# Linear attention and a factored bilinear layer in one kernel: a second raw-weight buffer, placed decoding steps, and another split of transfers between two queues

## The chip, the cores and the metric

One core of one Trainium2 chip runs the whole program. The metric is the device time of one execution in microseconds (us); the median of several runs is compared. Beside it stands one execution taken with the hardware profiler, from which all rows below come. PE is the matrix engine (TensorE), PEld its weight loads, DVE the vector engine, ACT the scalar engine, POOL is GpSimd; SPq and POOLq are the instruction queues of SyncE and GpSimd, from which this kernel starts nearly all its DMAs.

## The reference

The inputs are float32: q, k, v of 8 batches x 8 heads x 576 positions x 64, the feature matrix w_phi (64 x 128), w_a and w_b (512 x 1536), w_out (1536 x 512). The maximum runs over the features of one position.

```python
def phi(x):
    proj = einsum('bhsd,df->bhsf', x, w_phi)
    proj = proj - max(abs(proj), axis=-1, keepdims=True)
    return concatenate([exp(proj), exp(-proj)], axis=-1)
q_p, k_p = phi(q), phi(k)
kv  = einsum('bhsf,bhsd->bhfd', k_p, v)
z   = sum(k_p, axis=2)
num = einsum('bhsf,bhfd->bhsd', q_p, kv)
den = einsum('bhsf,bhf->bhs', q_p, z)[..., None] + 1e-06
attn = num / den                      # 8 x 8 x 576 x 64
...
x = attn as 4608 tokens x 512
y = ((x @ w_a) * (x @ w_b)) @ w_out   # 4608 x 512
```

The three weight matrices come in as float64 values seen as integers: each raw tile holds 64-bit words, which the kernel decodes to float32 by itself.

## The kernel before

**Attention.** 32 steps, one for each pair of heads of a batch, run through a software pipeline: while pair i is projected (`project_first`, `project_last`), pair i-1 goes through `kv_products` and pair i-2 through `num_products` and `den_products`. ACT takes the exponentials (L138, L139, L173, L174) and the copies out of PSUM (`p` L152 and L165, `back` L198, `x` L216, `dn` L227). The normalised result goes to DRAM as `xnorm`.

**Decoding of weights.** `load_factors` treats one unit, a 256-row piece of w_a, w_b or w_out. There are 18 units: 9 for the first pass of what follows, which `early` decodes between the steps of attention, and 9 for the second pass, which `late` decodes during the first pass, from its second block on. A unit loads two raw tiles of 512 KB (`raw_00a` and so on: pass, quad, matrix; L323), one after the other into one buffer. Each is decoded by one ACT operation (L328) and four on DVE (L329, L331, L333, L335) into `w32`. Out of `w32` come the seven factors of a Winograd-like scheme (w11, w12, s2, s1, s3, w22, s4), each split into a high part (ACT, L87) and a low part (DVE, L88) in a tile `t` of two buffers, from which a DMA of 256 KB (L349) stores it to DRAM as `kept`. Loads and stores go through SyncE in the early half, through GpSimd in the late half. Of a decoding step, only this is fixed: it comes behind the last operation that was put in the list `marks`, which are DVE operations (`placed`). The rates DECODE_RATE and LAST_RATE say how many steps are drawn at each turn of attention and at each product of a pass.

**The two passes.** The second half computes y transposed, in two passes p over halves of the inner dimension. A pass goes over 6 blocks j of 768 tokens, a block over 3 quads q. For a quad, `winograd` does seven products for w_a and w_b, each of 6 matmuls for each of the two (two chunks, three products of high and low parts), and multiplies the two results; then `product` in `moe_block` does seven products with w_out, each of 3 matmuls for each quad and each half. That is 3 x 7 x 2 x 6 = 252 matmuls with w_a and w_b and 7 x 3 x 2 x 3 = 126 with w_out in a block, each of 128 x 128 by 384 columns: 378, and 4536 in all. Pass 0 stores its partial sums (`part`, L538) in DRAM, pass 1 loads them again (L532) and stores `out_x`.

**The ring.** Weight factors come back from `kept` in pairs of 512 KB (`back_w`, `back_s`, `back_o`; `fetch`, L374) into a ring of four tiles. Each fetch is drawn by `feed` behind a product and waits for the tile's earlier product. Of the 11 pairs of w_out factors of a pass, 10 stay on chip and one goes through the ring in each block, at its end. All those fetches, the loads of x (`xx`, L390), `part` and `out_x` go through SyncE, in the order of issue.

**What sets the order.** The Tile framework schedules every operation by an estimate of its own; `issue_after` (in `behind`) gives only a lower bound. On each engine and in each DMA queue the resulting order is then fixed, and a waiting instruction holds all that stand behind it.

Of the kernel before, what the change touches and what calls it, by code (L numbers as in the profile page):

```python
# [18 lines left out]
P = 128  # L19
# [6 lines left out]
DECODE_FROM, DECODE_RATE = 3, 1.22  # L26
X_FROM, X_RATE = 100, 0.8
LAST_FROM, LAST_RATE = 1, 1.45
# [7 lines left out]
def tile_kernel(ctx, tc, qP, km, kr, vm, vr, w_phi, eye, w_a, w_b, w_out, out):  # L36
# [56 lines left out]
    marks, loads, feeds, maxima, st = [], [], [], [], {}  # L93
# [35 lines left out]
    def features(u, y, n, a1, a2):  # L129

        p = y if n == NFULL else y[:, :, :F]
        p = p.rearrange("p j (c f) -> p j c f", f=F)
        d = a2.tile([P, 2, n, F], F32, tag=f"d{n}", name=f"d_{u}")
        m = a2.tile([P, 2, n], F32, tag=f"m{n}", name=f"m_{u}")
        nc.vector.tensor_reduce(out=m, in_=p, op=ALU.max, axis=AX.X, apply_absolute_value=True)
        marks.append(nc.vector.tensor_tensor(d, p, m.unsqueeze(3).broadcast_to([P, 2, n, F]), op=ALU.subtract))
        e = a1.tile([P, 2, n, 2, F], F32, tag=f"e{n}", bufs=2, name=f"e_{u}")
        nc.scalar.activation(e[:, :, :, 0], d, AF.Exp)  # L138
        nc.scalar.activation(e[:, :, :, 1], d, AF.Exp, scale=-1.0)  # L139
        return e  # L140
# [18 lines left out]
    def project_last(i, a1, a2, consts, duo):  # L159
        p32 = st["p", i]  # L160
        x = q_half(i, 1, consts, duo)
        if i % 2 == 0:
            for j in range(2):
                mm(x[:, j, HALF : HALF + F], st["rk", i][heads[j]], consts[0][heads[j]])
        nc.scalar.copy(p32[:, :, times[1]], x[:, :, :HALF])  # L165
        if i % 2 == 0:
            st["er", i] = st["er", i + 1] = features(f"r_{i}", x[:, :, HALF:], 1, a1, a2)
        eq = a1.tile([P, 2, 2, S], F32, tag="eq", bufs=3, name=f"eq_{i}")
        for j in range(2):
            mb = a2.tile([P, S], F32, tag="mb", name=f"mb_{i}_{j}")  # L170
# [3 lines left out]
        nc.scalar.activation(eq[:, :, 1], p32, AF.Exp, scale=-1.0)  # L174
        st["eq", i] = eq
# [125 lines left out]
    late_o = [(NQ - 1, k) for k in FACTORS[:2]]  # L301
    late_o += [(q, k) for k in FACTORS for q in range(NQ) if (q, k) not in late_o]
    outs = [[(p, q, "o", k) for q, k in late_o] for p in range(2)]
# [8 lines left out]
    def load_factors(p, q, nm):  # L312

        n = DM // 2
        w32 = coded.tile([P, 4, n], F32, tag="w32", name=f"w32_{p}{q}{nm}")
        w = w32.rearrange("p i n -> p (i n)")
        src = {"a": w_a, "b": w_b, "o": w_out}[nm]
        for i in range(2):
            f = 2 * (NQ * p + q) + i
            raw = coded.tile([P, DM, 2], U32, tag="raw", name=f"raw_{p}{q}{nm}{i}")  # L320
            queue = nc.gpsimd if p else nc.sync
            rows = src[f * P : (f + 1) * P, :].bitcast(U32)
            behind(maxima if p else [], lambda: queue.dma_start(raw.rearrange("p n w -> p (n w)"), rows))  # L323
            yield
            low, high = raw[:, :, 0], raw[:, :, 1]
            g, s = high.bitcast(F32), w[:, i * DM : (i + 1) * DM]
            gb, sb = g.bitcast(U32), s.bitcast(U32)
            nc.scalar.activation(g, high.bitcast(F32), AF.Prelu, scale=2.0**-112, alpha=2.0**32)  # L328
            nc.vector.tensor_scalar(sb, gb, 3, None, op0=ALU.logical_shift_left)  # L329
            yield  # L330
            nc.vector.tensor_scalar(gb, sb, 0xFF800000, None, op0=ALU.bitwise_and)  # L331
            yield
            nc.vector.scalar_tensor_tensor(g, low, 2.0**-52, g, op0=ALU.mult, op1=ALU.mult)  # L333
            yield
            nc.vector.tensor_tensor(s, s, g, op=ALU.add)  # L335
            yield
        at = dict(w11=0, w12=1, w21=2, w22=3)
        if nm == "o":
            at.update(w12=2, w21=1)

        def stored(*names):
            for k in names:
                key, place = two[p, q, nm, k]
                t = coded.tile([P, 2, n], F32R, tag="t", bufs=2, name=f"t_{p}{q}{nm}_{k}")
# [4 lines left out]
                queue.dma_start(kept[key][:, place], t.bitcast(F32))  # L349

        def sub(k, a, b, to, op=ALU.subtract):
            at[k] = at[to]
            nc.vector.tensor_tensor(w32[:, at[k]], w32[:, at[a]], w32[:, at[b]], op=op)

        stored("w11", "w12")
        yield
        stored("w22")
        yield
        sub("s1", "w21", "w22", "w22", op=ALU.add)
        stored("s1")  # L360
        yield
        sub("s3", "w11", "w21", "w21")
        sub("s2", "s1", "w11", "w11")
        yield
        stored("s3")
        sub("s4", "w12", "s2", "w12")
        yield
        stored("s2", "s4")
        yield

    def fetch(key, pool, tag, name):
        n = len(pairs[key])
        t = pool.tile([P, n, 2, DM // 2], F32R, tag=tag, name=f"back_{name}")
        feeds.append(nc.sync.dma_start(t.bitcast(F32), kept[key][:, :n]))  # L374
        weights[key] = t

    def factors_of_x(p, j, xs):
# [4 lines left out]
        for c in range(half):  # L382
# [3 lines left out]
            while t < (j + 1) * T:  # L386
# [3 lines left out]
                behind(feeds or loads, lambda: nc.sync.dma_start(x32[:, :, t0 : t0 + m], rows))  # L390
# [12 lines left out]
        for c in range(half):  # L403
            (x11, x12), (x21, x22) = ((t[:, :N], t[:, N:]) for t in (x[c], x[c + half]))
            sums = xin.tile([P, 2, N], F32, tag="xs", name=f"xs_{u}_{c}")
            t1, t2, t3, t4 = sums[:, 0], sums[:, 1], x12, x21
# [21 lines left out]
    def winograd(p, j, q, xs, hs, spaces, feed):  # L428
# [32 lines left out]
        def hi(k, src):  # L461
            hs[k] = [spaces["h"].tile([P, N], F32R, tag=f"h{part}_{q}_{k}", name=f"h{part}_{k}_{u}") for part in "hl"]
            nc.scalar.copy(hs[k][0], src)  # L463
# [30 lines left out]
        h21 = low[:, 1]  # L494
# [6 lines left out]
        t1, t2, t3, t4 = top0[:, 1], top1[:, 1], low[:, 0], top0[:, 0]  # L501
# [16 lines left out]
    def moe_block(p, j, xs, x_next, spaces, feed, spent):  # L518
# [9 lines left out]
        def given_tile(i, t):  # L528
            g = spaces["brief"].tile([P, 2, N], F32, tag=f"g{(0, 1, 2, 0)[2 * i + t]}", name=f"o_{p}_{j}_{i}{t}")
            given.update({(m, i, t): g[:, m] for m in range(2)})  # L530
            if p:
                behind(feeds, lambda: nc.sync.dma_start(g, src[:, i * (NCC // 2) : (i + 1) * (NCC // 2), t * N : (t + 1) * N]))  # L532
# [4 lines left out]
        def store(key):  # L537
            nc.sync.dma_start(dst[at(*key)], given[key])  # L538
# [21 lines left out]

        early, late_, every = range(NQ - 1), range(NQ - 1, NQ), range(NQ)
        for q in range(NQ):
            for _ in range(3 if q == 0 else 2):
# [4 lines left out]
                if q == 1:  # L568
                    next(x_next, None)
            if q < NQ - 1:  # L570
                next(quads[q + 1])
                if q == 1:
                    next(x_next, None)
# [7 lines left out]
            if q == 0:  # L581
                next(x_next, None)
            if q == 1:
                for i, t in ((0, 0), (0, 1), (1, 0)):
# [10 lines left out]
        spent()  # L595
# [24 lines left out]
        for m in range(2):  # L620
            product(m, "w22", 0, every)
            if p:
# [12 lines left out]
    def placed(steps):  # L635

        for _ in iter(lambda: behind(marks, lambda: done.append(next(steps, steps))), 0):
            if done.pop() is steps:
                return
            yield  # L640

    done = []
    units = [(p, q, nm) for p in range(2) for q in range(NQ) for nm in "ab"]
    units = [[u for u in units if u[0] == p] + [(p, q, "o") for q in range(NQ)] for p in range(2)]
    codes = [itertools.chain(*(load_factors(*u) for u in units[p])) for p in range(2)]
# [5 lines left out]
    order = deque(key for p in range(2) for _ in range(NB) for key in [(p, *key) for key in order] + [("o", p, 0)])  # L651
    ring, used = deque(f"ring{i}" for i in range(RING)), [0]

    def refill():
        key = order.popleft()
        fetch(key, ringed, ring[0], "_".join(map(str, (used[0], *key))))
# [12 lines left out]
    early, late = (placed(code) for code in codes)  # L669

# [21 lines left out]
    wouts = ctx.enter_context(tc.tile_pool(name="wouts", bufs=1))  # L692
    for p in range(2):
        own = deque(pair for pair in pairs if pair[:2] == ("o", p) and pair[2])

        def feed():
# [4 lines left out]
            if own and used[0] % 3:  # L701
                key = own.popleft()
                fetch(key, wouts, f"o{key[2]}", "_".join(map(str, key)))

# [3 lines left out]
        for j in range(NB):  # L708
            n_ = p * NB + j + 1
            x_next = factors_of_x(*divmod(n_, NB), xs) if n_ < 2 * NB else iter(())  # L710
            moe_block(p, j, xs, x_next, spaces, feed, lambda: refill() if order else None)
# [46 lines left out]
```

## Time and profile before

| | |
|---|---|
| median of 3 runs | 1321.12 us (1317.03 to 1327.0) |
| profiled execution, whole | 1316.53 us |
| its span in the trace | 1314.4 us |
| attention, about | 0 to 418 us |
| pass 0, about | 418 to 864 us |
| pass 1, about | 864 to 1312 us |
| PE busy | 1156.3 us (88%) |
| DVE / ACT / POOL busy | 929.7 / 632.9 / 187.1 us (71 / 48 / 14%) |
| TensorE clock granted, mean | 0.963 of 2.4 GHz |

The span runs from the first to the last instruction that the profiler shows; 2.1 us of the execution lie around it. Busy shares are means over three stages that differ.

### The profile page before, as it was taken

How to read it: one execution, taken by the hardware profiler on the slowest of the kernel's cores; microseconds unless marked ns; L12 is line 12 of the kernel's file. 1: busy time of each engine (PE TensorE's matmuls, PEld its weight loads, DVE VectorE, ACT ScalarE, POOL GpSimd, SP SyncE). 2: the span in 40 equal slices, each digit the busy share in tenths (PEclk: the TensorE clock that was granted, in tenths of full speed). 3: DMA queues.
4: the chain of work that ended last, by engine and by line, in shares of the span. 5: the costliest groups of instructions: out<-in, count | busy, mean ns of one | idle time of the engine just before them, and what ended most of it. 6: DMA issues, size and time to landing. Idle time of an engine off the chain costs nothing. (4 is left out here: it accounts for less than half of the span.)

```text
span 1314.4 us, 22642 instructions
## 1 busy us (share of the span) xinstructions
PE 1156.3 (88%) x8418; PEld 1005.5 (76%) x8418; DVE 929.7 (71%) x1774; ACT 632.9 (48%) x1239; POOL 187.1 (14%) x149
## 2 busy tenths in 40 slices
PE   8787878787878789798898989989998999898998
PEld 5454545444545689798898889889998999898998
DVE  6776677678973475977959597865858585767655
ACT  6665557566754243544535354443525352433432
POOL 4333244233321000111101111100000000000000
PEclk9998899889999899999999999999999999999999
DMA  6576565667552966868777787979676777768573
GB/s 205 184 242 201 168 201 176 190 191 218 174 162 88 334 223 216 304 217 307 257 256 258 246 294 265 322 238 315 205 246 225 229 252 217 244 199 270 179 216 126
DMA packets 131645, 297.77 MB, mean 227 GB/s; under 512 B 22800, under 2 KB 53904, under 8 KB 131536
## 3 DMA queue, kind: packets, MB, share of 16 engines
q1 hardware_dynamic: 123600, 270.24, 62.9%
q0 software_dynamic: 7632, 25.96, 5.3%
q8 instruction: 67, 1.10, 0.4%
q14 instruction: 42, 0.34, 0.1%
q10 hardware_dynamic: 304, 0.13, 0.0%
HBM read 234.64 MB, written 61.64 MB: 225 GB/s over the span
## 5 line engine op out<-in xcount | busy, mean ns | idle before, releaser
L171 POOL PARTITION_ALL_REDUCE mb<-p x64 | 142.2, 2264 | 258.8 <-ACT p L165 222.7
L426 PE MATMUL po<-hh_s,back_o 128*128 128x384 f32 x576 | 161.6, 339 | 2.8 <-ACT hh_s L463 2.2
L426 PE MATMUL po<-hh_w,back_o 128*128 128x384 f32 x432 | 121.7, 338 | 13.4 <-DMA back_o<-kept_o 13.3
L426 PEld LDWEIGHTS po<-hh_s,back_o 128*128 128x128 f32 x576 | 106.4, 190 | 5.7 <-ACT hh_s L463 3.1
L426 PE MATMUL po<-hl_s,back_o 128*128 128x384 f32 x288 | 97.4, 338 | 2.0 <-DVE hl_s L466 2.0
L426 PEld LDWEIGHTS po<-hh_w,back_o 128*128 128x128 f32 x432 | 79.4, 189 | 16.3 <-DMA back_o<-kept_o 15.9
L535 DVE TENSOR_TENSOR o<-po,o 128x384 f32<-128x384 f32 x84 | 45.7, 553 | 43.7 <-PE po L426 34.2
L463 ACT CAST hh_s<-top 128x384 fp32r<-128x384 f32 x72 | 36.9, 514 | 78.1 <-DVE top L502 72.2
L426 PE MATMUL po<-hl_w,back_o 128*128 128x384 f32 x216 | 72.6, 336 | 0.0
L78 PE MATMUL kv<-e,v 128*64 128x256 f32 x512 | 70.0, 421 | 1.1 <-ACT e L139 1.1
L78 PE MATMUL pn<-eq,kvh 128*64 128x288 f32 x512 | 69.4, 414 | 0.0
L78 PE MATMUL pk<-w,k 64*128 64x128 f32 x512 | 41.4, 308 | 29.3 <-ACT x L216 29.3
L78 PEld LDWEIGHTS pk<-w,k 64*128 64x128 f32 x512 | 37.9, 214 | 38.1 <-ACT x L216 36.2
L78 PE MATMUL pq<-q,w 64*128 64x288 f32 x256 | 52.5, 489 | 16.4 <-ACT dn L227 12.7
L426 PE MATMUL pa<-xs1h,back_s 128*128 128x384 f32 x144 | 45.0, 350 | 17.0 <-DMA back_s<-kept_s 14.7
L78 PEld LDWEIGHTS kv<-e,v 128*64 128x64 f32 x512 | 37.2, 151 | 28.9 <-issue 12.7
L459 DVE TENSOR_TENSOR top<-pa,top 128x384 f32<-128x384 f32 x72 | 39.8, 553 | 27.5 <-PE pa L426 25.2
L426 PEld LDWEIGHTS po<-hl_s,back_o 128*128 128x128 f32 x288 | 54.8, 190 | 2.9 <-DVE hl_s L466 2.9
L426 PE MATMUL pa<-xs3h,back_s 128*128 128x384 f32 x144 | 45.5, 357 | 12.0 <-ACT top L455 10.3
L249 DVE TENSOR_TENSOR x<-x,rb 128x576 f32<-128x576 f32 x32 | 33.5, 1048 | 31.3 <-DMA rb<-rec 26.8
L172 DVE TENSOR_TENSOR p<-p,mb 128x576 f32<-128x576 f32 x64 | 53.2, 831 | 2.1 <-POOL mb L171 2.0
L78 PEld LDWEIGHTS pn<-eq,kvh 128*64 128x64 f32 x512 | 34.0, 137 | 26.2 <-issue 6.1
(348 smaller groups left out, 3264.5 us busy)
## 6 DMA issues: line engine op xcount, KB each, us to landing
back_s<-kept_s SPq DMA_DIRECT2D x144, 512.0 KB
back_w<-kept_w SPq DMA_DIRECT2D x108, 512.0 KB
back_o<-kept_o SPq DMA_DIRECT2D x30, 512.0 KB
q<-in_qP SPq DMA_DIRECT2D x32, 288.0 KB
rb<-rec SPq DMA_DIRECT2D x64, 144.0 KB
xnorm<-x SPq DMA_DIRECT2D x32, 288.0 KB
xx<-xnorm SPq DMA_DIRECT2D x16, 576.0 KB
part<-o SPq DMA_DIRECT2D x48, 192.0 KB
```

Source lines behind the costliest of these rows:

```text
L78: return pe(lambda: nc.tensor.matmul(out, w, x, start=start, stop=stop, skip_group_check=True))
L171: maxima.append(nc.gpsimd.partition_all_reduce(mb, p32[:, j], P, bass_isa.ReduceOp.absmax))
L172: nc.vector.tensor_tensor(p32[:, j], p32[:, j], mb, op=ALU.subtract)
L249: behind(marks, lambda: nc.vector.tensor_tensor(x32, x32, rb, op=ALU.mult))
L426: issued[0] = nc.tensor.matmul(*args, skip_group_check=True, **kwargs)
L459: nc.vector.tensor_tensor(to[:, i], acc[k][i], to[:, i], op=ALU.add)
L463: nc.scalar.copy(hs[k][0], src)
L535: nc.vector.tensor_tensor(given[key], x, given[key], op=ALU.add)
```

## The change

- The early half's raw tiles get two buffers (pool `a2`), and two loads are drawn ahead; a buffer's next load is drawn as soon as its tile is decoded. The late half keeps one buffer, with three empty steps between the two tiles of a unit.
- `placed` puts a step also behind the last ACT operation of a new list `acts`: the second exponentials (L139, L174) and the copies `hs` of `hi` (L463).
- A step stores one factor at most (15 steps to a unit in the early half, 18 in the late half). DECODE_RATE goes from 1.22 to 1.12, LAST_RATE from 1.45 to 1.6.
- The tile `t` of the late half is now one buffer, tag `g2` (before: two). The early half's has two, as before.
- `h21` gets a tile of its own, and the temporary `t2` takes its place in `low`, so `top1` is held less long. In `factors_of_x` a difference is written over x11.
- All 11 pairs of w_out factors stay on chip; none goes through the ring.
- In the passes only the ring's fetches stay on SyncE. Loads of x (but for the first block's), `part`, `out_x` and the fetches of w_out factors go through GpSimd. The loads of x for a block are drawn at the start of the block before, and `given_tile` (1, 0) is made later in pass 0.

```diff
+    def raw_tiles(p, place, bufs):
+        for q, nm in units:
+            for i in range(2):
+                f = 2 * (NQ * p + q) + i
+                raw = place.tile([P, DM, 2], U32, tag="raw", bufs=bufs, name=f"raw_{p}{q}{nm}{i}")
...
+                behind(maxima if p else [], lambda: queue.dma_start(raw.rearrange("p n w -> p (n w)"), rows))
+                yield raw
...
+    def load_factors(p, place, stage):
+        ahead = 1 if p else 2
+        tiles = raw_tiles(p, place, ahead)
+        raws = deque(itertools.islice(tiles, ahead))
+        for _ in range(3):
+            yield
+        for q, nm in units:
...
+                nc.vector.tensor_tensor(s, s, g, op=ALU.add)
+                raws.extend(itertools.islice(tiles, 1))
+                yield
+                if p and i == 0:
+                    for _ in range(3):
+                        yield
...
+            stored("w11")
+            yield
+            stored("w12")
+            yield
...
-        feeds.append(nc.sync.dma_start(t.bitcast(F32), kept[key][:, :n]))
+        queue.dma_start(t.bitcast(F32), kept[key][:, :n])
...
-                behind(feeds or loads, lambda: nc.sync.dma_start(x32[:, :, t0 : t0 + m], rows))
+                if p or j:
+                    nc.gpsimd.dma_start(x32[:, :, t0 : t0 + m], rows)
+                else:
+                    behind(loads, lambda: nc.sync.dma_start(x32[:, :, t0 : t0 + m], rows))
...
-        h21 = low[:, 1]
+        h21 = spaces["brief"].tile([P, N], F32, tag="h21", name=f"h21_{u}")
...
-        t1, t2, t3, t4 = top0[:, 1], top1[:, 1], low[:, 0], top0[:, 0]
+        t1, t2, t3, t4 = top0[:, 1], low[:, 1], low[:, 0], top0[:, 0]
...
-            nc.sync.dma_start(dst[at(*key)], given[key])
+            nc.gpsimd.dma_start(dst[at(*key)], given[key])
...
-    order = deque(key for p in range(2) for _ in range(NB) for key in [(p, *key) for key in order] + [("o", p, 0)])
+    order = deque(key for p in range(2) for _ in range(NB) for key in [(p, *key) for key in order])
...
+        while True:
+            with ExitStack() as c:
+                for what in (marks, acts):
+                    if what:
+                        c.enter_context(tc.issue_after(what[-1].ins))
+                if next(steps, steps) is steps:
+                    return
+            yield
...
+        early = placed(load_factors(0, a2, lambda name: a2.tile([P, 2, DM // 2], F32R, tag="t", name=name)))
...
+    late = placed(load_factors(1, coded, lambda name: spaces["brief"].tile([P, 2, N], F32R, tag="g2", name=name)[:, :, : DM // 2]))
```

In the pieces of the order below a name ends in numbers: `raw_01a1` is raw tile 1 of quad 1's w_a for pass 0, `part_81<-o_0_2_11` a store of block 2's sums, `back_63_0_0_s1` the 63rd fetch, for pass 0, quad 0, factor s1.

**ACT in attention, about pair 8.** Before, the raw tile's ACT operation (L328) stands right ahead of the copies `x32` and `dn`:

```order
L139 ACTIVATE e_r_8_1105<-d_r_8_1101 128x2x128
L87 CAST t_01a_w11_1283<-w32_01a_1031 128x256
L87 CAST t_01a_w12_1288<-w32_01a_1031 128x256
L198 COPY back_7_1159<-kv_7_1128 128x384
L328 ACTIVATE raw_01a1_1164<-raw_01a1_1164 128x512
L216 COPY x32_6_1177<-pn_6_1168 128x576
L227 COPY dn_6_1197<-pd_6_1188 128x288
```

After, on the same engine and in the same place of the pipeline (the operation is L337 now):

```order
L174 ACTIVATE eq_8_1105<-p32_8_1062 128x2x576
L337 ACTIVATE raw_01a0_757<-raw_01a0_757 128x512
L165 COPY p32_9_1196<-pq_9_1_1227 128x2x288
L138 ACTIVATE e_9_1214<-d_9_1210 128x8x128
L139 ACTIVATE e_9_1214<-d_9_1210 128x8x128
L337 ACTIVATE raw_01a1_889<-raw_01a1_889 128x512
L198 COPY back_8_1278<-kv_8_1247 128x384
```

Each raw operation now stands right behind a second exponential (L174, L139), and the tiles lie in two buffers.

**SyncE's queue at the end of block 2 of pass 0, before.** Stores of `part` stand between the fetches of the ring:

```order
L374 DMA back_63_0_0_s1_6593<-kept_0_0_s1_456 128x1024
L538 DMA part_81<-o_0_2_00_6397 128x384 x2
L374 DMA back_66_0_1_w12_6828<-kept_0_1_w12_1291 128x1024
L374 DMA back_65_0_1_w11_6799<-kept_0_1_w11_1286 128x1024
L374 DMA back_68_0_0_s4_6874<-kept_0_0_s4_565 128x1024
L538 DMA part_81<-o_0_2_11_6607 128x384
L374 DMA back_67_0_0_w22_6847<-kept_0_0_w22_431 128x1024
```

After, GpSimd's queue has them, between the stores of the decoded factors (L361 now) and the loads of x (L406):

```order
L318 DMA raw_11b0_6227<-in_w_b 128x1024
L406 DMA xx_0_4_0_6753<-xnorm5_78 128x2x384
L406 DMA xx_0_4_0_6753<-xnorm6_79 128x2x384
L406 DMA xx_0_4_1_6756<-xnorm5_78 128x2x384
L406 DMA xx_0_4_1_6756<-xnorm6_79 128x2x384
L361 DMA kept_1_1_w22_6293<-t_11a_w22_6290 128x2x256
L556 DMA part_81<-o_0_2_00_6399 128x384 x2
L361 DMA kept_1_1_s1_6299<-t_11a_s1_6296 128x2x256
L556 DMA part_81<-o_0_2_11_6593 128x384 x2
L556 DMA part_81<-o_0_2_10_6713 128x384
L361 DMA kept_1_1_s3_6322<-t_11a_s3_6319 128x2x256
```

SyncE's queue has only fetches there now, and a store of a factor can stand behind a store of `part`. Before, GpSimd's queue had only raw loads and stores of factors there.

**GpSimd's queue in block 0 of pass 1, after.** The last stores and fetches of w_out factors stand among `out_x`:

```order
L389 DMA back_o_1_7_9384<-kept_o_1_7_7943 128x1024
L556 DMA out_x<-o_1_0_00_9519 128x384 x2
L361 DMA kept_o_1_4_7949<-t_12o_s2_8851 128x2x256
L550 DMA o_1_0_11_9712<-part_81 128x2x384
L389 DMA back_o_1_4_9288<-kept_o_1_4_7949 128x1024
L361 DMA kept_o_1_10_8904<-t_12o_s4_8901 128x2x256
L389 DMA back_o_1_10_9487<-kept_o_1_10_8904 128x512
```

Before, this queue was empty in pass 1, and the decoding was done by the end of pass 0; now the last two factors are stored and fetched in the middle of pass 1's first block.

## Rows read from the trace of the kernel before

**Rows 1.** Windows by stage: us; PE, PEld, DVE, ACT, POOL busy; PEclk, DMA, GB/s.

```profile
0.00:418.00 418.00, 335.26 (x3874) 206.38 (x3878) 300.56 (x478) 258.16 (x416) 142.94 (x69) 0.93 0.59 187
418.00:864.00 446.00, 396.59 (x2182) 383.18 (x2175) 328.88 (x701) 199.82 (x450) 44.15 (x80) 0.97 0.76 264
864.00:1312.00 448.00, 424.43 (x2372) 415.89 (x2370) 300.28 (x596) 174.89 (x374) 0.00 (x0) 0.98 0.70 227
493.00:567.00 74.00, 66.03 (x368) 65.14 (x367) 54.27 (x116) 33.77 (x75) 7.57 (x14) 0.95 0.71 249
```

**Rows 2.** Waits of PE in attention: us in total, times, longest.

```profile
PE pt L204 <- ACT back L198: 29.5, 20, 3.6
PE pk L78 <- ACT x L216: 29.3, 15, 5.2
PE pq L78 <- ACT dn L227: 12.7, 9, 3.1
```

**Rows 3.** Timeline, 106 to 108 us, ACT and PE: start, duration, idle before.

```profile
106.38 0.65 ACT L328 ACTIVATE raw_01a<-raw_01a 128x512 f32<-128x512 f32 x1 [6.39 <-DMA raw_01a<-in_w_a]
107.61 0.80 PE L78 MATMUL pk<-w,k 64*128 64x128 f32 x4 [5.22 <-ACT x L216]
```

**Rows 4.** Waits of ACT in attention; of raw and t the first and the last.

```profile
ACT eq L173 <- DVE p L172: 17.2, 15, 6.2
...
ACT raw_01a L328 <- DMA raw_01a<-in_w_a: 9.4, 2, 6.4
...
ACT t_01o_s L87 <- DMA kept_o<-t_01o_s: 4.9, 2, 4.6
...
ACT t_01o_w L87 <- DMA kept_o<-t_01o_w: 0.5, 1, 0.5
ACT raw_00a L328 <- DMA raw_00a<-in_w_a: 0.3, 1, 0.3
```

**Rows 5.** Waits of PE for DMAs in pass 0 behind its first block.

```profile
PE pa L426 <- DMA back_s<-kept_s: 12.9, 12, 2.8
PE po L426 <- DMA back_o<-kept_o: 12.0, 5, 5.4
PE pa L426 <- DMA back_w<-kept_w: 3.3, 3, 1.6
```

**Rows 6.** Waits of PE in pass 1.

```profile
PE pa L426 <- ACT top L455: 9.7, 6, 3.1
PE pa L426 <- DMA back_w<-kept_w: 4.8, 6, 1.5
PE pa L426 <- ACT low L455: 3.7, 2, 2.1
```

**Rows 7.** Timeline of SyncE's queue at 589 us, and of PE at 607.

```profile
589.13 7.68 SPq L538 DMA_DIRECT2D part<-o  x5
596.91 3.01 SPq L374 DMA_DIRECT2D back_s<-kept_s  x3
606.95 0.55 PE L426 MATMUL pa<-xs1h,back_s 128*128 128x384 f32 x1 [2.80 <-DMA back_s<-kept_s]
```

**Rows 8.** Timeline of ACT and PE in pass 1, block 3.

```profile
1132.33 0.51 ACT L87 CAST xw11h<-xx 128x384 fp32r<-128x384 f32 x1 [1.98 <-DMA xx<-xnorm]
1142.62 0.44 PE L426 MATMUL pa<-xs3h,back_s 128*128 128x384 f32 x1 [3.14 <-ACT top L455]
```

**Rows 9.** A late tile t by engine (ns min/median/max); then landing of all kept_s.

```profile
L87 ACT CAST t_11b_w<-w_11b x3: 404/407/408, 634.7 to 647.0; 128x256 fp32r<-128x256 f32 x3
L88 DVE TENSOR_TENSOR t_11b_w<-w_11b,t_11b_w x3: 419/420/426, 640.1 to 647.5; 128x256 fp32r<-128x256 f32 x3
L349 POOL DMA_DIRECT2D kept_w<-t_11b_w x3: 539/539/539, 641.1 to 648.2; - x3
...
DMA to landing us min/median/max: 2.3/4.8/6.7
```

**Rows 10.** Waits of SyncE's queue in blocks 1 to 11.

```profile
SPq L538 <- DVE o L535: 86.4, 53, 13.8
```

More of the change, by code (lines that the diff above doesn't have):

```diff
@@ L310, in weight @@
         return weights[key][:, i]
-    def load_factors(p, q, nm):
-        n = DM // 2
[L315 to L323, printed above, removed]
-            yield
[L325 to L344, printed above, removed]
@@ new lines, in raw_tiles @@
+    def raw_tiles(p, place, bufs):
[3 more added lines that the diff above has]
+                raw = place.tile([P, DM, 2], U32, tag="raw", bufs=bufs, name=f"raw_{p}{q}{nm}{i}")
+                rows = {"a": w_a, "b": w_b, "o": w_out}[nm][f * P : (f + 1) * P, :].bitcast(U32)
+                queue = nc.gpsimd if p else nc.sync
+                behind(maxima if p else [], lambda: queue.dma_start(raw.rearrange("p n w -> p (n w)"), rows))
+                yield raw
@@ L348, in stored, with sub, fetch @@
                     kept[key] = dpool.tile([P, 2, 2, n], F32, name="kept_" + "_".join(map(str, key)))
[L349 to L371, printed above, removed]
+                (nc.gpsimd if p else nc.sync).dma_start(kept[key][:, half], t.bitcast(F32))
+            def sub(k, a, b, to, op=ALU.subtract):
+                at[k] = at[to]
+                nc.vector.tensor_tensor(w32[:, at[k]], w32[:, at[a]], w32[:, at[b]], op=op)
+            stored("w11")
+            yield
+            stored("w12")
+            yield
+            stored("w22")
+            yield
+            sub("s1", "w21", "w22", "w22", op=ALU.add)
+            stored("s1")
+            yield
+            sub("s3", "w11", "w21", "w21")
+            sub("s2", "s1", "w11", "w11")
+            stored("s3")
+            yield
+            sub("s4", "w12", "s2", "w12")
+            stored("s2")
+            yield
+            stored("s4")
+            yield
+    def fetch(key, pool, tag, name, queue):
         n = len(pairs[key])
         t = pool.tile([P, n, 2, DM // 2], F32R, tag=tag, name=f"back_{name}")
-        feeds.append(nc.sync.dma_start(t.bitcast(F32), kept[key][:, :n]))
+        queue.dma_start(t.bitcast(F32), kept[key][:, :n])
         weights[key] = t
@@ L559, in product @@
                     in_turn(False, acc[m, to], w_, h_, **f)
+        for _ in range(NCC):
+            next(x_next, None)
         early, late_, every = range(NQ - 1), range(NQ - 1, NQ), range(NQ)
@@ L621, in moe_block @@
             product(m, "w22", 0, every)
+            if not p and m == 0:
+                given_tile(1, 0)
             if p:
@@ L635, in placed @@
     def placed(steps):
-        for _ in iter(lambda: behind(marks, lambda: done.append(next(steps, steps))), 0):
-            if done.pop() is steps:
-                return
+        while True:
[5 more added lines that the diff above has]
+                    return
             yield
[L642 to L645, printed above, removed]
+    units = [(q, nm) for q in range(NQ) for nm in "ab"] + [(q, "o") for q in range(NQ)]
     order = [(0, k) for k in FACTORS[:2]]
@@ L655, in refill @@
         key = order.popleft()
-        fetch(key, ringed, ring[0], "_".join(map(str, (used[0], *key))))
+        fetch(key, ringed, ring[0], "_".join(map(str, (used[0], *key))), nc.sync)
         ring.rotate(-1)
@@ L692, in tile_kernel @@
     wouts = ctx.enter_context(tc.tile_pool(name="wouts", bufs=1))
+    late = placed(load_factors(1, coded, lambda name: spaces["brief"].tile([P, 2, N], F32R, tag="g2", name=name)[:, :, : DM // 2]))
     for p in range(2):
-        own = deque(pair for pair in pairs if pair[:2] == ("o", p) and pair[2])
+        own = deque(pair for pair in pairs if pair[:2] == ("o", p))
         def feed():
@@ L702, in feed @@
                 key = own.popleft()
-                fetch(key, wouts, f"o{key[2]}", "_".join(map(str, key)))
+                fetch(key, wouts, f"o{key[2]}", "_".join(map(str, key)), nc.gpsimd)
             if p == 0 and j >= LAST_FROM:
```

55 lines of the change are left out of this document (31 added, 24 removed).

## The prediction

> **What bounds the kernel now.** I read the windows by stage first [rows 1]. Attention takes 418 us with PE busy for 335, DVE for 301 and ACT for 258: no engine is full, so the stage runs on waits. The passes take 446 and 448 us; PE is idle for 446 - 397 = 49 us in pass 0 and 448 - 424 = 24 us in pass 1, 73 together, and is the bound there. At the granted clock the passes also lose (1 - 0.97) x 446 + (1 - 0.98) x 448, about 22 us, against full speed.
>
> Next come the waits of PE, stage by stage. In attention three kinds make 29.5 + 29.3 + 12.7 = 71.5 us, all of them for an ACT copy [rows 2]. Such a copy is short; what makes it late stands ahead of it on ACT. The timeline shows it once: ACT stands 6.39 us for a raw weight tile, and PE stands 5.22 us for the copy that follows [rows 3]. The waits of ACT itself then say how much of this there is: nine rows of it for raw tiles (from 9.4 us down to 0.3) add up to 41.7 us, and 21 rows in which a cast into `t` waits until an older `t` has been stored (from 4.9 down to 0.5) to 45.9 us [rows 4]. Together 87.6 us, of which PE shows 71.5: a microsecond of decode wait on ACT costs PE 71.5/87.6 = 0.82. So attention is bound by decoding, not by its own arithmetic.
>
> In the passes the waits of PE are for transfers: 12.9 + 3.3 us for the ring's weights in pass 0 behind its first block, 12.0 for w_out factors there [rows 5], 4.8 in pass 1, where 9.7 + 3.7 for an eviction by ACT are the larger share [rows 6]. The cause of the first kind is seen in SyncE's queue: five stores of partial sums hold it for 7.68 us, three fetches leave only behind them, and PE then stands 2.80 us [rows 7].
>
> **The change part by part.** The sum is made against the profiled execution, 1316.5 us; the median lies 4.6 above it, which is added at the end.
>
> *Raw tiles in attention.* With two buffers a load starts when the tile two before it has been decoded, not the last one, and each tile's ACT operation stands behind a long exponential. A load that ACT waited 6.39 us for at the worst [rows 3] then has the decoding of a whole tile, several steps, to land. I take all 41.7 us of raw waits away: 0.82 x 41.7 = 34 us. The waits for `t` keep two buffers, but with one factor for each step no two casts stand side by side (they did: t_01a_w11 and w12 in the order); I take a fifth of 45.9, 0.82 x 9 = 7.5. Together -42. What is late next is `eq`, which waits 17.2 us for DVE [rows 4]. The ends: half of the raw waits turn into others, 0.82 x 21 = -17; or all of the raw's 34 and half of the `t` waits (0.82 x 23 = 19) go, and the granted clock of 0.93, which costs 0.07 x 418 = 29 us there, gives a third back (10), -63.
>
> *w_out out of the ring.* The 12.0 us of waits for `back_o` behind block 0 [rows 5] go, -12, and each block has one 512 KB fetch less in the ring. The ends: -12 to -6, if the next weight is late instead.
>
> *SyncE left to the ring.* Waits for `back_s` and `back_w` outside block 0 are 12.9 + 3.3 + 4.8 [rows 5, 6] and 0.5 more in pass 1, 21.5. Not all stem from the queue: a fetch must also wait for a ring tile, and the DMA engines are 0.70 to 0.76 busy [rows 1]. I take half, -11 (ends 0 and -20).
>
> *Clock.* PE fell to a lower granted clock behind gaps. Of 73 us of idle time in the passes, 12 + 11 + 7 = 30 go by these terms, so of 22 us I take 30/73, -9 (ends 0 and -15).
>
> *x ahead, `top1` freed earlier.* In pass 1 ACT waits 1.98 us for a load of x, and 10 us later PE waits 3.14 us for the eviction of `top1` behind it on ACT [rows 8]. With the load a block ahead the first goes; but the casts of x and the three `hh_s` still stand ahead of the eviction, only one `hh_w` went behind it. Of 9.7 + 3.7 [rows 6] I take half, -7 (ends 0 and -12).
>
> *Block 0 of pass 0.* All w_out pairs are fetched through GpSimd beside the ring, which was already so but for one pair and the queue: 0, +-5.
>
> *Overhang.* The last two w_out factors are stored and fetched in block 0 of pass 1, behind `out_x` in GpSimd's queue; s2 of quad 2 needs them near the block's end. Nothing in the trace shows this. The nearest rows are the longest wait for `back_o`, 5.4 [rows 5], and the longest hold of a queue by such stores, 13.8 [rows 10]; landing takes 4.8 twice [rows 9]. The ends are 0 and 13.8 + 9.6, about +23; I take +8, nearer the first row, since two thirds of a block lie between.
>
> *One late `t`.* A cast must wait until the tile before it has been cast (0.41), subtracted (0.42), issued by GpSimd (0.54) and landed (4.8 median): 6.2 us [rows 9]. In the changed order 441 instructions of ACT lie from the first to the last of the 63 late casts, 7.1 for each of 62 links. ACT did 75 in a block of 74 us, 0.99 us each [rows 1], so a link has 7.0 us. It fits on the mean, but 19 links have five instructions or fewer, and by 6.2 less 0.99 for each they are short by 40 us in all. Pass 0 has such waits already and PE hardly shows them, so I take +5 (ends -5, since steps no longer come in pairs, and +30).
>
> The sum: -42 - 12 - 11 - 9 - 7 + 0 + 8 + 5 = -68, which makes 1248.5, and 1253 for the median.
>
> **The rivals.** *The single late `t` sets the pace of pass 0 (slower).* Stores of factors now stand behind stores of `part` on GpSimd, and ACT is in order: a late landing holds the next cast, and all copies that PE needs behind it. With the slowest landing, 6.7, a link is 6.7 + 0.41 + 0.42 + 0.54 = 8.1 us; a store of `part` held its queue for 86.4/53 = 1.6 us on the mean [rows 10], and half of that in each link gives 8.9. Each of 63 links then outlasts its 7.0 us by 1.9: +120 in place of the +5, so -73 + 120 = +47, and 1368. It decides the sign where a link takes 7.0 + 73/63 = 8.2 us. For it speaks that two buffers became one while the queue got busier; against it that the median landing leaves 0.8 us.
>
> By the Trainium skill ("DMA: Bandwidth & Descriptors", section "Anatomy of one DMA — SWDGE (gpsimd) path") a transfer from GpSimd takes about 2.0 us plus its bytes over 436,000 for each us, which is an estimate of 2.6 us for 256 KB. The trace does not bear this out, at a median of 4.8 us with the ring running beside it [rows 9]; by the page a link would take 4.0 us and this rival would be out, by the trace it stays in.
>
> *Attention hardly gains.* The loop has 32 steps of 13 us, in which DVE works 9.4 and ACT 8.1 [rows 1]; if its own chain (17.2 us of `eq` waiting for DVE, [rows 4]) stands right behind the decode waits, -10 instead of -42: 1253 + 32 = 1285. For it speaks that many copies wait in a row; against it that PE's waits match ACT's in place and size [rows 3].
>
> *The queue was not the reason.* The waits for `back_s`, `back_w` and `back_o` come from DMA engines that both queues share, 0.71 to 0.76 busy [rows 1]. Moving transfers to another queue moves no bytes; the waits (12 + 11) stay and with them 7 us of clock: 1253 + 30 = 1283. Against it speaks the held queue [rows 7].
>
> The Trainium skill speaks for this one ("DMA: Bandwidth & Descriptors", section "SWDGE vs HWDGE vs iDMA"): inside each DMA engine the two kinds of queues are separate and the engine goes round between them, so a fetch of the ring no longer stands ahead of a store but shares with it. No row of before shows the two side by side without a held queue, so its chance rests on [rows 1] alone.
>
> **How the numbers follow.** The forecast, 1253, has 0.50, and its own terms put it between about 1215 and 1285. Attention hardly gaining, 1285, has 0.20; the shared engines, 1283, 0.20; the single `t`, 1368, 0.10. If both middle cases came, 1253 + 32 + 30 = 1315 would be no change. A measurement of this kernel can tell about 1% from nothing. The range 1210 to 1302 holds the first three cases but for their tails, and leaves out the last. Faster by over 1% is below 1308: 0.50 + 0.20 + 0.20 less 0.08 for tails, 0.82. Within 1%: 0.08. Slower: 0.10.
>
> **What would show it.** Right: no row of ACT waiting for a raw tile in attention, which ends near 376 us; no wait for `back_o` in the later blocks of pass 0; SyncE's rows of waits for DVE gone, and GpSimd's in their place. Wrong: attention still above 400 us with PE waiting for ACT or DVE; waits for `back_s` as before; ACT waiting for `kept` in pass 0 over 60 us, with PE waiting behind it; a wait for `back_o` of several us in the first block of pass 1.

## The result, and the profile after

The changed kernel takes 1338.87 us (median of 12 runs, 1328.56 to 1350.69), the kernel before 1320.62 (median of 12): a ratio of 1.0112, 95% interval 1.0083 to 1.0141. A gain of 5% was forecast, and the change costs 1%. The profiled execution took 1331.85 us, span 1329.4 us, at the low end of its runs. The runs compared are undisturbed ones, so the ratio lies a little under that of the medians.

The windows by stage are the first view again (us; PE, PEld, DVE, ACT and POOL busy with their counts; PEclk, DMA share, GB/s), now cut where attention, pass 0 and pass 1 end in the changed kernel:

```profile
0.00:421.00 421.00, 336.24 (x3882) 207.69 (x3882) 292.17 (x478) 258.95 (x416) 144.02 (x73) 0.92 0.58 189
421.00:889.00 468.00, 420.15 (x2274) 405.11 (x2275) 334.92 (x703) 202.98 (x456) 97.16 (x153) 0.97 0.72 246
889.00:1327.00 438.00, 404.86 (x2264) 397.56 (x2262) 293.98 (x593) 168.13 (x368) 68.04 (x109) 0.98 0.67 223
```

Pass 1 begins here with ACT's first eviction for it, at 889 us. In the kernel before that eviction stands at 887, where [rows 1] end pass 0 at 864, some 23 us early. Measured in this way, pass 0 took 468 us before as well, and pass 1 about 423 to PE's last matmul, against 433 after. So nothing was gained in attention and pass 0, and pass 1 lost 10 us.

**Attention.** ACT's waits for raw tiles, 41.7 us before, are gone: no row of them is left. Those for `t` are 52.8 us, where they were 45.9. PE waits as long as in [rows 2], for ACT again; its waits in attention (engine, line and releaser; us in total, times, longest):

```profile
PE pt L204 <- ACT back L198: 45.9, 19, 7.1
PE pk L78 <- ACT x L216: 19.7, 8, 4.2
PE pn L78 <- ACT eq L173: 6.4, 1, 6.4
```

That is 72.0 us, where three rows made 71.5. On ACT, `eq` now waits for DVE 37.4 us where it waited 17.2 [rows 4], and DVE waits in turn for the reciprocals that come back from DRAM; the first row of DVE's waits after, which was 18.8 us in 9 times before:

```profile
DVE x L249 <- DMA rb<-rec: 32.5, 11, 4.6
```

The timeline of DVE shows what stands behind such a wait: a low part of `t`, which has to be done before the tile is stored and ACT may cast into it again.

```profile
214.53 1.56 DVE L249 TENSOR_TENSOR x<-x,rb 128x576 f32<-128x576 f32 x1 [3.31 <-DMA rb<-rec]
...
216.08 0.41 DVE L88 TENSOR_TENSOR t_02a_w<-w_02a,t_02a_w 128x256 fp32r<-128x256 f32 x1
```

**Pass 0.** The waits for transfers did get shorter. Before, PE waited 20.9 + 12.0 + 8.8 us for `back_s`, `back_o` and `back_w` in the whole pass; after, 13.7 for `back_w`, 0.2 for `back_s` and nothing for `back_o`. But its waits for ACT went from 5.0 us in all to 25.9, and all its waits together only from 50.9 to 47.8. The first waits of PE, 421 to 889 us:

```profile
PE pa L443 <- DMA back_w<-kept_w: 13.7, 8, 4.2
PE po L443 <- ACT hh_s L480: 10.6, 7, 2.7
PE po L443 <- ACT o L561: 5.0, 7, 3.7
PE pa L443 <- ACT low L472: 4.3, 2, 2.6
```

ACT was late since it stood for stores of the single late `t`: 62.2 us in 32 waits there, 32.8 in 16 before.

**Pass 1, first block.** ACT's row first, then two of PE (timeline: start, duration, idle before and its releaser):

```profile
948.29 0.40 ACT L87 CAST t_12o_s<-w_12o 128x256 fp32r<-128x256 f32 x1 [4.43 <-DMA kept_o<-t_12o_s]
...
952.66 0.69 PE L443 MATMUL pa<-xs2h,back_s 128*128 128x384 f32 x1 [6.74 <-ACT top L472]
...
964.68 0.69 PE L443 MATMUL po<-hh_s,back_o 128*128 128x384 f32 x1 [6.21 <-DMA back_o<-kept_o]
```

The cast of one of the last factors holds ACT, so `top` is evicted late. 12 us later PE needs the factor itself. Its fetch left GpSimd only at 957.5 us, when its store had landed and behind a load of `part` that had waited 5.64 us for `out_x`. In the run not only the last two factors but the whole last unit, seven of them, was cast in pass 1 (908 to 957 us). The two gaps are 13 us, and the granted clock (PEclk, third from the end, as a share of 2.4 GHz) is low behind them, as two windows with the columns above show:

```profile
965.00:975.00 10.00, 10.00 (x47) 10.00 (x47) 2.23 (x4) 1.44 (x3) 1.28 (x2) 0.78 0.21 68
975.00:985.00 10.00, 10.00 (x60) 10.00 (x59) 6.03 (x12) 1.00 (x2) 4.04 (x7) 1.00 0.51 153
```

PE is busy without a gap in both, and does 47 matmuls in the first and 60 in the second.

### The profile page after: what moved, and what is told of

It is laid out like the page before. It is cut to its first block, busy times and chain, and to the rows that moved or that the text cites. A ratio compares the mean times of both kernels' runs of the same rounds, so it can differ in the third digit from the quotient of the medians.

```text
span 1329.4 us, 22626 instructions
## 1 busy us (share of the span) xinstructions
PE 1161.2 (87%) x8418; PEld 1010.4 (76%) x8418; DVE 921.1 (69%) x1774; ACT 630.1 (47%) x1239; POOL 309.2 (23%) x335
## 5 line engine op out<-in xcount | busy, mean ns | idle before, releaser
L443 PE MATMUL po<-hh_s,back_o 128*128 128x384 f32 x576 | 168.4, 348 | 24.2 <-ACT hh_s L480 10.6
L443 PEld LDWEIGHTS po<-hh_s,back_o 128*128 128x128 f32 x576 | 109.3, 196 | 30.1 <-ACT hh_s L480 12.8
L480 ACT CAST hh_s<-low 128x384 fp32r<-128x384 f32 x108 | 55.1, 512 | 37.2 <-DVE low L523 20.9
L406 POOL DMA_DIRECT2D xx<-xnorm x44 | 31.4, 717 | 165.8 <-DVE xs4l L88 161.5
L553 DVE TENSOR_TENSOR o<-po,o 128x384 f32<-128x384 f32 x84 | 45.0, 553 | 32.5 <-PE po L443 23.4
L78 PE MATMUL kv<-e,v 128*64 128x256 f32 x512 | 65.8, 401 | 1.3 <-ACT e L139 1.3
L483 DVE TENSOR_TENSOR hl_s<-low,hh_s 128x384 fp32r<-128x384 f32 x108 | 57.5, 553 | 7.5 <-ACT hh_s L480 7.5
L204 PE MATMUL pt<-ident,back 128*128 128x128 f32 x96 | 19.0, 310 | 50.0 <-ACT back L198 45.9
L443 PE MATMUL pa<-xw11h,back_w 128*128 128x384 f32 x144 | 45.3, 356 | 18.9 <-DMA back_w<-kept_w 16.4
L204 PEld LDWEIGHTS pt<-ident,back 128*128 128x128 f32 x96 | 10.6, 148 | 65.3 <-ACT back L198 63.6
```

The source lines that it names most:

```text
L78: return pe(lambda: nc.tensor.matmul(out, w, x, start=start, stop=stop, skip_group_check=True))
L204: pe(lambda: nc.tensor.transpose(pt[:, g], back[:, g], consts[1]))
L406: nc.gpsimd.dma_start(x32[:, :, t0 : t0 + m], rows)
L443: issued[0] = nc.tensor.matmul(*args, skip_group_check=True, **kwargs)
L480: acts.append(nc.scalar.copy(hs[k][0], src))
L483: marks.append(nc.vector.tensor_tensor(hs[k][1], src, hs[k][0], op=ALU.subtract))
```

## The experiments

Each kernel is the changed one but for the edit named; e9 and e13 are the kernel before. In the profile of each, "attention ends" is PE's first matmul of pass 0 (for e1, where PE then waits for decoded weights, the end of attention's last matmul), and "passes" is the time from there to the end of PE's last matmul. "Whole" is the median of the runs, with the ratio to the kernel before; e1, e2, e3, e10 and e13, which have no ratio, are one execution each.

| run | attention ends | passes | whole, ratio (95%) |
|---|---|---|---|
| before / after | 419.4 / 421.3 | 891.1 / 901.2 | 1320.6 / 1338.9 |
| e1 decode behind attention | 361.8 | | 1406.8 |
| e2 four early t | 411.4 | 901.6 | 1322.0 |
| e3 later reciprocals | 396.5 | 898.5 | 1304.0 |
| e4 late decoding from block 0 | 428.9 | 882.7 | 1326.7, 1.0069 (1.0037 to 1.0101) |
| e5 = e2 + e3 | 381.7 | 897.7 | 1296.0, 0.9792 (0.9729 to 0.9855) |
| e6 two late t, h21 back | 431.7 | 882.1 | 1320.4, 0.9981 (0.9949 to 1.0014) |
| e7 h21 back | 433.8 | 899.1 | 1337.8, 1.0098 (1.0058 to 1.0138) |
| e8 x, part, out_x on SyncE | 431.2 | 898.8 | 1335.1, 1.0082 (1.0052 to 1.0112) |
| e9 before + later reciprocals | 405.2 | 878.9 | 1291.1, 0.9767 (0.9727 to 0.9806) |
| e10 steps not behind `acts` | 424.0 | 883.1 | 1316.0 |
| e11 = e5 + e4 | 380.7 | 886.0 | 1275.9, 0.9627 (0.9558 to 0.9696) |
| e12 = e3 + three early t + e6 | 385.6 | 877.5 | 1276.3, 0.9661 (0.9608 to 0.9714) |
| e13 before, again | 426.0 | 891.9 | 1323.9 |
| e14 = e5, one raw buffer | 387.7 | 892.8 | 1290.2, 0.9767 (0.9695 to 0.9839) |
| e15 = e12 + e4 | 386.6 | 868.4 | 1266.1, 0.9578 (0.9520 to 0.9636) |

**What attention waits for.** Theory A: the decode's waits on ACT. Theory B: the reciprocals' transfers. Run e1 takes the decoding out of attention.

```diff
-DECODE_FROM, DECODE_RATE = 3, 1.12
+DECODE_FROM, DECODE_RATE = 1000, 1.12
```

> The changed kernel with the decoding of pass 0's weights drawn only behind attention, so that attention runs alone and the decoding alone behind it. Theory A (decoding is what attention waits for, in ACT's order): attention, 421 us in the changed kernel, ends near 345 (421 less the 76 us that PE waits for ACT and DVE), with no wait of PE for the copy back over a few us. Theory B (attention's own chain of reciprocals, four transfers one behind the other on SyncE, stands right behind the decode waits): attention still takes 395 to 415, with DVE waiting for rb. The whole gets longer by the decoding, which then stands by itself.

It ended at 362, between the two: with no decoding DVE waits 81 us for `rb`. Against the five profiles of the changed kernel's attention (421 to 434, see e13) the decoding costs 60 to 72 us, and with the reciprocals where they are no more than that can be had from it.

```diff
-    ... a2.tile([P, 2, DM // 2], F32R, tag="t", name=name)
+    ... a2.tile([P, 2, DM // 2], F32R, tag="t", bufs=4, name=name)
```

> The changed kernel with four buffers in place of two for the early half's t. Theory A (ACT's waits for the storing of t, 52.8 us in attention, are passed on to PE by 0.8): these waits fall under 10 us and attention ends at 380 to 390 in place of 421. Theory B (the reciprocals' transfers set the pace): the waits for t go too, but DVE's wait for rb grows from 32.5 us and attention ends at 412 or later.

Theory B, but for half a microsecond: ACT's waits for `t` fell from 52.8 to 3.2 us, DVE's for `rb` rose to 64, and attention ended at 411.4.

```diff
-REC_TURNS, REC_LATER = (1, 3, 4, 5, 7, 8), 4
+REC_TURNS, REC_LATER = (1, 4, 5, 7, 10, 11), 4
...
-        for t in range(4 * (NP + LAG), 4 * (NP + LAG) + 10):
+        for t in range(4 * (NP + LAG), 4 * (NP + LAG) + 14):
```

> The changed kernel with the steps of the reciprocals later (turns 1, 4, 5, 7, 10, 11 in place of 1, 3, 4, 5, 7, 8). Theory B: DVE's wait for rb (32.5 us) and ACT's wait for p from DVE (37.4) fall to a third, and attention ends at 395 to 405. Theory A: attention stays at 415 to 421, since ACT still waits some 50 us for t.

Theory B again, at 396.5. ACT's wait for `p` fell less than expected, from 37.4 us to 20.9. The row of DVE's waits that was 32.5 us:

```profile
DVE x L249 <- DMA rb<-rec: 5.3, 1, 5.3
```

> The changed kernel with both edits to attention: four early buffers t and the later reciprocals. Theory B (two chains side by side, the storing of t and the reciprocals' transfers, each hiding the other): where each alone ended attention at 411 and 396, both together end it at 375 to 385, with ACT's waits for t under 10 us and DVE's for rb under 25; whole 1290 to 1305 if the passes stay at their 901 us. Rival: attention's rest is DVE and PE work, so the second edit adds nothing and it ends at 393 to 398.

Both edits, 381.7, as Theory B had it: each chain had hidden part of the other. ACT's waits for `t` are 4.1 us now and DVE's for `rb` 8.9, but `eq` still waits 33.3 us for DVE; that wait did not set attention's length.

The kernel before with the later reciprocals alone, to see what the raw buffer is worth:

> The kernel before, one raw buffer and all, with only the later reciprocals. Theory B (two chains side by side): here the decode waits, 87.6 us on ACT, are still there, so attention stays at 410 to 419 and the whole within 1%; only with the second raw buffer do the later reciprocals give the 25 to 35 us that they gave in the changed kernel. Rival: the reciprocals alone were the bound and the raw buffer is worth nothing, attention ends at 395 to 400, the whole at 1298 to 1304.

Here Theory B's claim for the raw buffer fell, and the rival's range was missed too. With nearly all the decode waits left (ACT still stands 30.4 us for raw tiles and 45.8 for `t`), attention ended at 405 and the whole at 1291, against 1304 in the one execution of the changed kernel with the same edit. So the two chains overlap only in part. Its passes also took 879 us against 891, which no theory here expected; the order in them shifts a little with the edit, and the cause stays open.

> The run with four early buffers t and the later reciprocals (attention 382 us, whole 1296), with one raw buffer in attention in place of two. Theory E (the second raw buffer is worth something once the reciprocals are out of the way): attention ends at 390 to 405, with ACT's waits for raw at 25 to 40 us again. Theory F (behind the exponentials, one buffer does): attention stays within 5 us of 382.

```diff
-        ahead = 1 if p else 2
+        ahead = 1
```

Nearer to Theory F, whose bound it misses by 1 us: with one buffer attention ends 6 us later and the whole is not slower. ACT's waits for raw tiles are 12.1 us, with one row over 2 us:

```profile
ACT raw_01a L337 <- DMA raw_01a<-in_w_a: 9.9, 1, 9.9
```

> The changed kernel with steps placed behind the last DVE mark only, no longer behind the last ACT operation of the list acts. Five executions of the changed kernel's attention, in the same order of instructions but for its end, took 421, 429, 431, 432 and 434 us, the kernel before 419. If the place behind the exponentials is what made it slower, attention ends at 405 to 420 here; if the reciprocals are, at 425 to 435.

```diff
-                for what in (marks, acts):
+                for what in (marks,):
```

424, between the two ranges. ACT's waits for raw tiles are back at 38.0 us, with two buffers, and DVE's for `rb` fall to 20.0. So it is mostly the place behind the exponentials, not the second buffer, that covers the loads; and covering them moved attention's end by some 10 us at most.

The edit also frees the late half's steps from the copies `hs`, and its passes took 883 us: pass 0 449 in place of 468, and pass 1 434, as in the changed kernel. The single late `t` is still there, and ACT stands 57 us for its stores in pass 0. Kernels with the same passes and other edits to attention took 892 to 901 us, so this place probably costs pass 0 some 10 us or more. That is one execution, and no run tests it apart.

> The kernel before, unchanged, once more: how far its stages vary. Attention took 419 us and the passes 891 in the one profile of it; the changed kernel's attention took 421 to 434 in five. If the change made attention slower, this one lies at 412 to 421; if attention merely varies, at 425 to 435.

426: attention varies by 7 us in the kernel before too. The changed kernel's five values (its own, e4, e6, e7 and e8), 421 to 434, lie some 7 us higher on the mean; with two values before that is not settled as a loss.

**What the passes wait for.** Theory C: the single late `t`. Theory D: GpSimd's queue, where factors stand behind `part` and `out_x`.

```diff
-LAST_FROM, LAST_RATE = 1, 1.6
+LAST_FROM, LAST_RATE = 0, 1.4
```

> The changed kernel with the late decoding from block 0 on, at 1.4 steps for each product in place of 1.6 from block 1 on, still with one buffer t. Theory C (the single late t: links too short for a landing, and the last factors in pass 1's first block): the waits of PE in pass 1's first block for top and back_o (6.7 and 6.2 us) go, and pass 0's waits for hh_s, o, low and top (some 20 us) shrink by a third; whole time 1310 to 1322 where the changed kernel has 1332 to 1339. Theory D (GpSimd's queue, where factors wait behind part and out_x): pass 0 stays as it is, only the overhang goes, 1320 to 1328.

The overhang went, and with it 18.5 us of the passes. In pass 1 PE has no row of a wait for `back_o` or `top` left. Pass 1 took 411 us in place of 433. But pass 0 took 471, and its waits for ACT stayed (24.1 us against 25.9), so this half of Theory C's expectation missed. The whole missed with it, as attention took 429. Taken alone the run came out as Theory D had it, 1320 to 1328.

The lines that this edit puts in:

```diff
+    turns = itertools.cycle((True, False))
+    def late_tile(name):
+        if next(turns):
+            return spaces["brief"].tile([P, 2, N], F32R, tag="g2", name=name)[:, :, : DM // 2]
+        return coded.tile([P, 2, DM // 2], F32R, tag="lt", name=name)
...
+        h21 = low[:, 1]
...
+        t1, t2, t3, t4 = top0[:, 1], top1[:, 1], low[:, 0], top0[:, 0]
```

> The changed kernel with two late buffers t, for whose room h21 goes back into low and t2 into top1. Theory C (the single late t is what pass 0 and pass 1's first block lose by): the passes take 875 to 888 us in place of 901, PE's waits for hh_s, o, top and low in pass 0 fall under 10 us and ACT's for kept by half; whole 1312 to 1326. Theory D (factors wait on GpSimd behind part and out_x): ACT's waits stay over two thirds, the passes take 895 or more.

Theory C. PE's waits for ACT in pass 0 are 8.8 us in all, ACT's for stores of `t` 27.5 in place of 62.2, and the last late factor is cast at 879 us, 16 before pass 1 begins. The waits of PE in pass 0 come first below. Then come the landings (min/median/max, us) of the stores of late factors of w_a and w_b: of the s factors, where the changed kernel has 2.5/4.4/8.8, and of the w factors, where it has 2.6/4.9/7.4.

```profile
PE pa L443 <- DMA back_w<-kept_w: 15.2, 8, 4.2
PE po L443 <- DVE hl_s L483: 7.4, 6, 1.7
PE po L443 <- ACT hh_s L480: 3.0, 5, 1.1
...
DMA to landing us min/median/max: 2.3/2.6/5.7
DMA to landing us min/median/max: 2.3/5.6/6.9
```

One median fell and the other rose. Over all 63 late stores the median is 4.8 us in the changed kernel, 4.4 here and 4.5 in e7, which has one buffer. So the stores hardly landed faster; ACT had a second tile to go on with.

> The changed kernel with only h21 back in low and t2 in top1, the control of the run before. If top1's earlier release is worth anything, PE's wait for top in pass 1 outside its first block rises from under 1 us towards the 9.7 of the kernel before, and the passes take 903 to 910; if the loads of x ahead did that, the passes stay at 899 to 903 and the whole at 1332 to 1340.

This is the control of e6: 899 us and 1338. With the steps placed as they are, the 17 us are thus the buffer's, 5.5 of them in pass 0 (468.5 against 463.0) and 11.5 in pass 1 (430.2 against 418.7). And `top` in pass 1 outside its first block stays at 0.9 us, so the earlier release of `top1` is worth nothing that shows. By the expectation the loads of x ahead then took the waits of [rows 6] away; no run tests them alone.

> The changed kernel with the loads of x, part and out_x back on SyncE; only the fetches of w_out stay on GpSimd. Theory D: the late stores of factors land sooner, pass 0's waits for hh_s, o, top and low fall under 10 us, and the passes take 880 to 890. Theory C: those waits stay within a third, the waits for back_s (0.2 us in pass 0) come back to 5 to 13, and the passes take 900 to 915, the whole 1335 to 1350.

```diff
-                    nc.gpsimd.dma_start(x32[:, :, t0 : t0 + m], rows)
+                    nc.sync.dma_start(x32[:, :, t0 : t0 + m], rows)
...
-            nc.gpsimd.dma_start(dst[at(*key)], given[key])
+            nc.sync.dma_start(dst[at(*key)], given[key])
```

For pass 0 Theory D is out: the passes took 898.8 us, and pass 0's waits for ACT are 23.8. Theory C's second half missed there as well: with the stores back on SyncE, `back_s` cost PE only 1.1 us in pass 0. In pass 1, though, the waits for `back_s` did come, 14.1 us against 3.5 in the changed kernel:

```profile
PE pa L443 <- DMA back_s<-kept_s: 14.1, 8, 3.7
```

So the sum hides two changes. Pass 0 took 476 us, against 468. Pass 1 took 422, where seven kernels with the overhang and with `out_x` on GpSimd took 430 to 447. No wait for `back_o` is left in it; but the last factor is also cast 51 us into pass 1, where the changed kernel casts it after 68, so that the queue did this is not shown. The waits for `back_s` in pass 0 of the kernel before may have come from the ring's extra fetch or from the place of the steps, or PE's waits for ACT may cover them here; none of these was tried apart.

**The versions that win.**

> The changed kernel with four early buffers t, the later reciprocals and the late decoding from block 0 on. If the pieces add: attention 382 and passes 883, 1265 and some 17 more, 1282; ratio to the kernel before 0.965 to 0.975. If the late steps in block 0 hurt there, 1285 to 1295.

> The changed kernel with three early buffers t, the later reciprocals, and two late buffers t with h21 back in low. If the pieces add: attention 382 to 388 and passes 882, 1282 to 1288; ratio 0.968 to 0.978.

> Three early buffers t, the later reciprocals, two late buffers t and the late decoding from block 0 on, all together. Each of the last two alone took some 17 us off the passes, by the same waits, so together they should add little: 1272 to 1280, within 0.5% of the two runs with one of them.

Both of the first two beat what the pieces add up to, and the third missed low: the passes took 868 where either cure alone gave 878 to 886, so the two cures are not the same gain. With the late decoding from block 0 on (e11) pass 0 took 473 us and pass 1 412, with the second buffer (e12) 461 and 416, with both (e15) 456 and 412. The windows of e15 by stage, in the columns of the first view:

```profile
0.00:387.00 387.00, 324.83 (x3884) 202.68 (x3885) 301.30 (x482) 259.75 (x417) 150.85 (x73) 0.95 0.65 206
387.00:843.00 456.00, 417.52 (x2275) 400.52 (x2274) 338.33 (x721) 204.57 (x464) 104.09 (x172) 0.98 0.78 266
843.00:1258.00 415.00, 397.61 (x2263) 390.91 (x2261) 287.36 (x572) 168.66 (x358) 55.76 (x90) 1.00 0.68 220
```

In pass 1 PE is busy for 398 of 415 us at a granted clock of 1.00; attention, with PE busy for 325 of 387, has the most idle time of PE left.

## Why the prediction was wrong

**The step that failed: attention.** "A microsecond of decode wait on ACT costs PE 0.82" was read from two sums that agree, 87.6 and 71.5 us. That they agree does not say that PE's waits go when ACT's do. The raw waits went (41.7 to 0), and PE's stayed (71.5 to 72.0). While ACT stood for a tile, the reciprocals made their round through DRAM unseen, and without that cover DVE stood for them: with raw waits of 0 it waits 32.5 us for `rb`, with 38.0 (e10) it waits 20.0. The -42 was about 0, as attention took 421 to 434 us against 419 and 426.

The runs put prices on the chains. Later reciprocals are worth 25 to 37 us against the five profiles of the same attention, 30 with four early `t` (e2 against e5), and 14 to 21 in the kernel before. The second raw buffer is worth 6 (e14 against e5), and 9 together with the new places of the steps (e9 against e3).

The rival "attention hardly gains" named the right place. It took `eq` for DVE as the chain's wait, which is still 33.3 us where attention ends at 382; the wait to name was DVE's for `rb`, a row of 18.8 us that the prediction did not show. The prediction gave the rival 0.20.

**The second step that failed: what the passes gain.** For w_out, the ring, the clock and x ahead together -39 was taken. With two late buffers (e6), which takes the single `t` and the overhang out again, the passes took 882 us against 891 and 892 before: some -9. The waits named did shrink. In pass 0 PE's waits for DMAs were 41.7 us before and are 17.6 in e6. But its waits for ACT and DVE rose from 9.2 to 19.1, so that all its waits fell by 11 us and pass 0 by 5. Pass 1 gained 4. A wait taken off PE's list was priced at its full length, and gave back a part of it; where the rest went stays open.

**The single late `t` and the overhang** were nearly of their size. +5 and +8 were taken; e6 against its control shows 5.5 us in pass 0 and 11.5 in pass 1. PE's waits for ACT in pass 0 grew by 21 in the changed kernel, but stood largely in the place of those for DMAs. The rival that made this buffer the bound of pass 0 asked for 120 us; ACT did stand for stores of `t`, 62.2 us against 32.8, but the rival's size was that of a landing of 6.7 us in every link, where the median of the 63 late stores is 4.8. Its ground in pass 0, factors waiting behind `part`, is out by e8.

**Right in the waits, not shown in the time:** w_out pairs out of the ring, as no wait for `back_o` is left in pass 0. **Right in pass 0, for a reason not shown:** the waits for `back_s` went almost whole (20.9 to 0.2), but those for `back_w` rose to 13.7, and by e8 the queue alone did not do it. **Mis-sized the safe way:** x ahead; of 13.4 us of waits for `top` and `low` in pass 1 [rows 6] 1.3 are left outside the overhang, where 7 were forecast to go. **The clock's 9 us** did not come: the mean granted clock fell from 0.963 to 0.954, and PE's waits in the passes, which were to shrink by 30 us, summed to 71.5 us before and 76.5 after.

The rival that moving a transfer to another queue gives nothing had a point in e8 (1335 against 1339), if only as the sum of a longer pass 0 and a shorter pass 1. The Trainium skill's rule beside it ("DMA: Bandwidth & Descriptors", section "SWDGE vs HWDGE vs iDMA"), that an engine goes round between the two kinds of queues, agrees with e8 as far as the sum goes; no row here shows the taking of turns itself.

The Trainium skill's 2.0 us plus one for each 436,000 bytes ("DMA: Bandwidth & Descriptors", section "Anatomy of one DMA — SWDGE (gpsimd) path"), an estimate of 2.6 us for 256 KB, is near the shortest landings here, 2.3 us in e6 and 2.5 in the changed kernel. The median of the 63 late stores is 4.4 in e6, 4.8 in the changed kernel and 4.9 before, so the estimate holds about as a floor and not as the price in a busy kernel.

## What to carry to other kernels

Where several chains stall one pipeline, two sums of waits that match do not make one the price of the other. Before costing a wait at its full length, look for the next row on the engine behind it (here 18.8 us of DVE for `rb`); here a single constant in the schedule moved it. Taking a buffer away costs time where a step must land before the next may start: compare the shortest links with the landing, not the mean. Work that overhangs a stage can cost twice, once through the engine that does it (PE waited 6.74 us for ACT here) and once where its result is first needed (6.21 us). And compare stage by stage: in e8 one pass lost about what the other gained.

## What was not expected of the hardware

Issuing a store of 256 KB took GpSimd 539 ns (median) in the kernel before, and 717 in the changed one, where the tile is a slice of a wider one. In e6, where every other tile is one of its own, most issues took 540 to 585 ns and 712 to 725 in turn, so the time goes with the slice; no run here says why. The landing of such a store does not go with the number of buffers: the s factors landed sooner in e6 than in the changed kernel (2.6 us against 4.4, medians) and the w factors later (5.6 against 4.9).
